# A windowed-attention, dense-layer and eight-expert kernel: row gathers issued three steps sooner, gate values copied out, 32-row tails computed in float32 in four column quarters, weight splits on VectorE alone

## The chip, the cores and the metric

The kernel runs on one core of a Trainium2 chip. The metric is the device time of one execution in microseconds; a kernel's time is the median of its runs. TensorE is written PE in the profile, its weight loads PEld, VectorE is DVE, ScalarE is ACT, GpSimd is POOL and SyncE, which issues most of the DMAs, is SP.

## What is computed

Three layers follow each other on 4 x 576 = 2304 tokens of width 512.

```
scores = scale * q @ k.T            # causal window of 64, softmax, @ v
x = concat of heads                 # [2304, 512]
h = x @ w_in                        # dense layer, width 2048
g = h * sigmoid(1.702 * h)
x = g @ w_out
logits = x @ w_gate                 # eight experts, the best one per token
gate_w = softmax(logits)[best]
for e in range(8):
    xe = x[best == e]
    out[best == e] = gate_w * (relu(xe @ w1[e]) @ w2[e])   # width 1024
```

All inputs and outputs are float32, and the kernel keeps nearly that precision: a float32 operand is split into a high part in the matmul type float32r and a low part, the rest, in the same type, and a product is made of three float32r matmuls (high by high, high by low, low by high).

## The kernel before

**Attention and the dense layer** fill the first 535 us or so, in nine chunks of 256 tokens; their order comes from a small planner with cost figures. While they run, each token's row (512 values of x, its gate value and its token number, 514 floats) is scattered into a buffer `xbuf` in DRAM, where each expert has its own stretch of rows.

**The experts** are the part that the change touches. The experts are taken in descending order of their number of tokens, with fixed room `CAPS` (L39) of 384, 352, 352, 288, 288, 256, 256 and 256 rows; below, "expert 3" is the fourth in that order. Which expert that is, is a value read at run time (`which`, L598). The room is cut into blocks of 128 rows (`blocks`, L595), so that experts 1 and 2 have a last block of 96 rows and experts 3 and 4 a last block of 32 rows.

For each expert, `load_rows` (L625) fetches its rows from `xbuf` into a tile `xg` by one DMA per block on the SP queue. There are two such tiles, one for even and one for odd experts (`xp2["go"[e % 2]]`, each with one buffer), so the rows of expert e+1 overwrite those of expert e-1. `rows_t` (L639) transposes a block on PE into `et` in PSUM, and ACT and DVE split it into `eh` and `el`; DVE also copies the token numbers into `ti` (L658). `load_expert` (L605) fetches an eighth of an expert's weights (512 KB) into a staging tile `ws`, of which there are four, and `prep_expert` (L620) splits half of such an eighth: ACT writes the high part (L150), and the low part (L151) is made on POOL for the first half and on DVE for the second. The split weights lie in tiles `whi` and `wlo` of the pool `wp`, eight of each (L69), that is two experts' worth.

`e_up` (L660) makes one of the eight 128-wide slices m of the hidden layer for all rows of the expert: 12 matmuls, whose moving operand has as many columns as the expert has rows. ACT makes `gh` from it (L681), and DVE makes `gl` (L682). `e_down` (L689) multiplies that slice by 128 rows of w2 and adds to one PSUM bank `o` per block, by three matmuls of 512 columns for each block, whatever the number of rows in the block (L162, L163 and L165). After slice 7, `e_out` (L707) scales each block by the gate value, which it reads in `xg` (L712), on ACT or, for block 1, on DVE, and scatters the rows to the output by an indirect DMA on POOL. The output tiles `os` come from a pool with three buffers (L67). PSUM has eight banks, one pool for all.

**The order** is written out by hand for PE alone (`manual_schedule`, L1025): PE runs the instructions in the order of the program. In the expert loop the other engines' queues and the DMA queue are ordered by the framework's scheduler, which follows the program's order where its own model says that an instruction is ready. The loop (L1068) has one step for each expert and slice; step (e, z) is

```
if i % NF == 0 and e + 1 < E:
    load_rows(e + 1)
e_up(*steps[i])
if i > 1:
    e_down(*steps[i - 2][0:2])
```

and after that come `rows_t` of expert e+1 for block z-2, `prep_expert` for eighth z of expert e+1, and `load_expert` two eighths further on. So `e_down` runs two steps behind `e_up`: slice 7 of expert e is finished in step (e+1, 1), its blocks are put out there, and the first transposes of the expert after next stand in step (e+1, 2). Expert 0 is special: seven of its slices were already made for its first 256 rows within the dense layer's end, and its first eight steps do the rest.

Of the kernel before, what the change touches and what calls it, by code (L numbers as in the profile page):

```python
# [9 lines left out]
F32 = mybir.dt.float32  # L10
# [3 lines left out]
U32 = mybir.dt.uint32  # L14
# [3 lines left out]
ALU = mybir.AluOpType  # L18
# [23 lines left out]
PAIR = 3  # L42
ROW = DM + 2
XB = (NT - CMIN) // P
NEG = -8.0e9
SKIP = 4096
Z_SCALE = 2.0**-29 * (1.0 - 2.0**-20)
# [4 lines left out]
def tile_model(  # L52
# [539 lines left out]
    ev_t = {}  # L592
    xp2 = {}

    def blocks(e):  # L595
        return [(b, min(P, CAPS[e] - b * P)) for b in range(-(-CAPS[e] // P))]

# [22 lines left out]
    def prep_expert(e, i, h, lo_eng):  # L620
        j, z = divmod(i, 2)
        hi, lo = ew_t[e, j]
        split(hi[:, 2 * z + h], lo[:, 2 * z + h], st_t[e, i][:, h], lo_eng)

    def load_rows(e, which_blocks=None):  # L625
        if e not in ex_t:
            ex_t[e] = [
                xp2["go"[e % 2]].tile([P, CAPS[0] // P, ROW], F32, tag="xg", name="xg", bufs=1),
                sm.tile([P, CAPS[0] // P], U32, tag="ti", name="ti"),
            ]  # L630
        xg = ex_t[e][0]
        for b, n in which_blocks or blocks(e):
            src = xbuf.rearrange("(e r) d -> e r d", e=E)[which(e), b * P : b * P + n, :]
            ins = nc.sync.dma_start(out=xg[0:n, b, :], in_=src.rearrange("o r d -> r (o d)"))
            for w in put[-2:]:
                tc.add_manual_dep(ins.ins, w.name, SYNC, reason="rows written before")
        return ins

    def rows_t(e, b):  # L639
        pool = xp2["go"[e % 2]]  # L640
        if b == 0:
            ex_t[e] += [
                pool.tile([P, KD, CAPS[0]], F32R, tag="eh", name="eh", bufs=1),
                pool.tile([P, KD, CAPS[0]], F32R, tag="el", name="el", bufs=1),
            ]
        xg, ti, eh, el = ex_t[e]
        n = blocks(e)[b][1]
        t = ps.tile([P, KD, P], F32, tag="ps", name="et")
        for k in range(KD):
            nc.tensor.transpose(  # L650
                t[:, k, 0:n], xg[0:n, b, k * P : k * P + P], ident[0:n, 0:n]
            )
        hv = eh[:, :, b * P : b * P + n]
        nc.scalar.activation(out=hv, in_=t[:, :, 0:n], func=AF.Copy)  # L654
        nc.vector.tensor_tensor(  # L655
            out=el[:, :, b * P : b * P + n], in0=t[:, :, 0:n], in1=hv.bitcast(F32), op=ALU.subtract
        )
        nc.vector.tensor_copy(out=ti[0:n, b : b + 1], in_=xg[0:n, b, DM + 1 : ROW])  # L658

    def e_up(e, m, c0=0, c1=None, skip=0):  # L660

        c1 = c1 or CAPS[e]
        n = c1 - c0
        hi, lo = ew_t[e, 2 * (m // 4)]
        f0 = (m % 4) * P
        xg, ti, eh, el = ex_t[e]
        h = ps.tile([P, 512], F32, tag="ps", name="eh_ps")[:, 0:n]
        for k in range(KD):
            mm3(
                h,  # L670
                (hi[:, k, f0 : f0 + P], lo[:, k, f0 : f0 + P]),
                (eh[:, k, c0:c1], el[:, k, c0:c1]),
                k == 0, k == KD - 1,
            )
        if "o" in xp2:
            pool, w, n_b = xp2["o"], CAPS[0], 3
        else:
            pool, w, n_b = gp, CH, 3
        gh = pool.tile([P, w], F32R, tag="gh", name="gh", bufs=n_b)[:, 0 : n - skip]
        gl = pool.tile([P, w], F32R, tag="gl", name="gl", bufs=n_b)[:, 0 : n - skip]  # L680
        nc.scalar.activation(out=gh, in_=h[:, skip:], func=AF.Relu)  # L681
        nc.vector.scalar_tensor_tensor(  # L682
            out=gl, in0=h[:, skip:], scalar=0.0, in1=gh.bitcast(F32), op0=ALU.max, op1=ALU.subtract
        )
        g_t["e", e, m] = (gh, gl, c0 + skip, c1)

    eo_t = {}

    def e_down(e, m):  # L689
        done, rows = [], []  # L690
        gh, gl, c0, c1 = g_t.pop(("e", e, m))
        hi, lo = ew_t[e, 2 * (m // 4) + 1]
        for b, n in blocks(e):
            if not c0 <= b * P < c1:
                continue
            if (e, b) not in eo_t:
                eo_t[e, b] = [ps.tile([P, DM], F32, tag="ps", name="o"), 0]
            o, i = eo_t[e, b]
            eo_t[e, b][1] += 1
            if i == NF - 1:  # L700
                done.append(b)
            rows.append((o[0:n], slice(b * P - c0, b * P - c0 + n), i == 0, i == NF - 1))
        mm3_rows(rows, (gh, gl), (hi[:, m % 4, :], lo[:, m % 4, :]))
        for b in done:
            e_out(e, b)

    def e_out(e, b):  # L707
        xg, ti = ex_t[e][0:2]
        n = blocks(e)[b][1]
        o = eo_t[e, b][0][0:n]  # L710
        os_ = yp.tile([P, ROW], F32, tag="ys", name="os")[0:n, 0:DM]
        gate = xg[0:n, b, DM : DM + 1]  # L712
        if b == 1:
            nc.vector.tensor_scalar(out=os_, in0=o, scalar1=gate, scalar2=None, op0=ALU.mult)
        else:
            nc.scalar.activation(out=os_, in_=o, func=AF.Copy, scale=gate)
        ins = nc.gpsimd.indirect_dma_start(  # L717
            out=out[:, :],
            out_offset=bass.IndirectOffsetOnAxis(ap=ti[0:n, b : b + 1], axis=0),
            in_=os_,  # L720
            in_offset=None,
            bounds_check=NT - 1,
            oob_is_err=False,
        )

        tc.declare_no_dep(ins.ins, group="out", reason="rows of their own")
        tc.add_to_no_dep_group("out", ins.ins)
# [297 lines left out]
    with tc.manual_schedule(engines={mybir.EngineType.PE}):  # L1025
        consts_attn()
        consts_gate()
        marks = {}
        for s in (slot[0, NM - 1], slot[0, NM - 1] - 3, LAST - 1, BEGIN, MEND):
            sched[s]  # L1030
        for s in sorted(x for x in sched if x < END1):
            if s == slot[0, NM - 1]:
                load_gate()
            if s == slot[0, NM - 1] - 3:
                with tc.issue_after(last_w[0].ins):
                    init_xbuf(yp.tile([P, ROW], F32, tag="ys", name="zt"))
            if s == LAST - 1:
                at_cm.__exit__(None, None, None)
                p2_cm = tc.tile_pool(name="p2g", bufs=2, reuse_waits="tile")
                xp2["g"] = p2_cm.__enter__()  # L1040
            if s == BEGIN:
                staged = tc.manual_schedule(
                    engines={
                        mybir.EngineType.Activation, mybir.EngineType.DVE, mybir.EngineType.Pool
                    }
                )
                staged.__enter__()
            if s == MEND:
                staged.__exit__(None, None, None)
            for _, fn in sorted(sched[s], key=lambda x: x[0]):  # L1050
                fn()
        xpool_cm.__exit__(None, None, None)
        yt_cm.__exit__(None, None, None)
        rows = load_rows(0, blocks(0)[2:])
        cnt, rank = pick_order()
        gp_cm.__exit__(None, None, None)
        p2o_cm = tc.tile_pool(name="p2o", bufs=1, side="right", reuse_waits="tile")
        xp2["o"] = p2o_cm.__enter__()
        for b, _ in blocks(0)[2:]:
            rows_t(0, b)  # L1060
        count_rows(cnt, rank)
        with tc.issue_after(rows.ins):
            for i in range(2):
                load_expert(1, i)
        steps = [(0, m, 0, CAPS[0], 0) for m in range(SPLIT, NF)]
        steps += [(0, m, CAPS[0] - 256, CAPS[0], 256 - (CAPS[0] - CH)) for m in range(SPLIT)]
        steps += [(e, m, 0, CAPS[e], 0) for e in range(1, E) for m in range(NF)]
        for i in range(E * NF + 2):  # L1068
            e = i // NF
            if e < E:  # L1070
                if i % NF == 0 and e + 1 < E:
                    load_rows(e + 1)
                e_up(*steps[i])
            if i > 1:
                e_down(*steps[i - 2][0:2])
            if e < E and e + 1 < E:
                z = i % NF
                if 0 <= z - 2 < len(blocks(e + 1)):
                    rows_t(e + 1, z - 2)
                prep_expert(e + 1, z, 0, nc.gpsimd)  # L1080
                prep_expert(e + 1, z, 1, nc.vector)
            if i + 2 < (E - 1) * NF:
                load_expert(*divmod(i + 2 + NF, NF))
        p2_cm.__exit__(None, None, None)
        p2o_cm.__exit__(None, None, None)
# [56 lines left out]
```

## Time and profile before

| | us |
|---|---|
| median of 3 runs (lowest to highest) | 769.55 (767.17 to 771.27) |
| the profiled execution | 768.63 |
| its span, first to last instruction | 766.9 |
| PE busy in the span | 730.2 (95%) |
| DVE, ACT, POOL busy | 477.5, 370.7, 171.2 |

The span is what the profile covers; 1.7 us of the profiled execution lie outside it. Busy time is the time in which at least one instruction of an engine was running. A matmul's end is modelled, and matmuls overlap, so the distance from one matmul's start to the next one's start says more than the mean duration.

### The profile page before, as it was taken

How to read it: one execution, taken by the hardware profiler on the slowest of the kernel's cores; microseconds unless marked ns; L12 is line 12 of the kernel's file. 1: busy time of each engine (PE TensorE's matmuls, PEld its weight loads, DVE VectorE, ACT ScalarE, POOL GpSimd, SP SyncE). 2: the span in 40 equal slices, each digit the busy share in tenths (PEclk: the TensorE clock that was granted, in tenths of full speed). 3: DMA queues.
4: the chain of work that ended last, by engine and by line, in shares of the span. 5: the costliest groups of instructions: out<-in, count | busy, mean ns of one | idle time of the engine just before them, and what ended most of it. 6: DMA issues, size and time to landing. Idle time of an engine off the chain costs nothing. (4 is left out here: it accounts for less than half of the span.)

```text
span 766.9 us, 14568 instructions
## 1 busy us (share of the span) xinstructions
PE 730.2 (95%) x5372; PEld 639.3 (83%) x5373; DVE 477.5 (62%) x1408; ACT 370.7 (48%) x965; POOL 171.2 (22%) x153
## 2 busy tenths in 40 slices
PE   5779999999999999999999999989999999999996
PEld 3669888888988898889888988868898888888895
DVE  5999866946764845936747538463765637265641
ACT  5999674444344344535443522451563526345520
POOL 2000011120112021011110110241554626255531
PEclk9899999999999999999999999999999999999998
DMA  9992278130222112211220000441862717437520
GB/s 343 385 383 92 101 271 289 37 101 18 84 74 100 41 49 86 73 37 65 74 100 1 1 28 1 141 135 42 282 230 98 271 56 250 164 115 264 189 68 24
DMA packets 43195, 98.97 MB, mean 129 GB/s; under 512 B 3823, under 2 KB 12015, under 8 KB 42864
## 3 DMA queue, kind: packets, MB, share of 16 engines
q1 hardware_dynamic: 40128, 88.54, 33.6%
q0 software_dynamic: 2992, 9.46, 3.2%
q8 instruction: 43, 0.70, 0.4%
q14 instruction: 32, 0.26, 0.1%
HBM read 82.22 MB, written 16.03 MB: 128 GB/s over the span
## 5 line engine op out<-in xcount | busy, mean ns | idle before, releaser
L155 PE MATMUL h<-xh,whi 128*128 128x256 f32 x576 | 166.0, 288 | 0.0
L157 PE MATMUL h<-xh,wlo 128*128 128x256 f32 x576 | 163.8, 284 | 0.1
L156 PE MATMUL h<-xl,whi 128*128 128x256 f32 x576 | 163.7, 284 | 0.0
L162 PE MATMUL y<-whi,gh 128*128 128x512 f32 x288 | 119.0, 413 | 5.0 <-ACT gh L397 5.0
L390 DVE SCALAR_TENSOR_TENSOR th<-th,h 128x256 f32<-128x256 f32 x144 | 60.1, 417 | 100.4 <-ACT th L386 99.5
L386 ACT ACTIVATE th<-h 128x256 f32<-128x256 f32 x144 | 54.7, 381 | 134.7 <-PE h L157 129.5
L155 PEld LDWEIGHTS h<-xh,whi 128*128 128x128 f32 x576 | 110.8, 192 | 6.2 <-ACT whi L364 0.3
L156 PEld LDWEIGHTS h<-xl,whi 128*128 128x128 f32 x576 | 110.8, 192 | 4.7
L163 PE MATMUL y<-wlo,gh 128*128 128x512 f32 x288 | 114.7, 398 | 0.0
L151 POOL TENSOR_TENSOR wlo<-ws,whi 128x512 fp32r<-128x512 f32 x64 | 94.3, 1485 | 87.5 <-ACT whi L150 82.9
L157 PEld LDWEIGHTS h<-xh,wlo 128*128 128x128 f32 x576 | 110.7, 192 | 0.5 <-DVE wlo L369 0.5
L151 DVE TENSOR_TENSOR wlo<-ws,whi 128x512 fp32r<-128x512 f32 x64 | 87.1, 1368 | 33.8 <-ACT whi L150 32.2
L238 POOL TENSOR_TENSOR pr<-pr,su 128x512 f32<-128x512 f32 x28 | 31.1, 1111 | 297.6 <-DVE su L236 177.7
L150 ACT ACTIVATE whi<-ws 128x512 fp32r<-128x512 f32 x128 | 74.4, 625 | 41.2 <-DMA ws<-in_w 40.8
L397 ACT ACTIVATE gh<-th 128x256 fp32r<-128x256 f32 x144 | 60.1, 417 | 65.2 <-DVE th L390 63.9
L165 PE MATMUL y<-whi,gl 128*128 128x512 f32 x288 | 90.7, 396 | 0.2
L447 DVE CUSTOM_DVE_ANT_0 junk<-ys,wg 128x512 bf16<-128x512 f32 x128 | 89.1, 696 | 2.7 <-DMA wg<-in_w_gateT 1.2
L155 PE MATMUL eh_ps<-eh,whi 128*128 128x256 f32 (+3 forms) x284 | 85.2, 300 | 0.7 <-ACT eh L654 0.7
L156 PE MATMUL eh_ps<-el,whi 128*128 128x256 f32 (+3 forms) x284 | 83.6, 294 | 0.3 <-DVE el L655 0.3
L157 PE MATMUL eh_ps<-eh,wlo 128*128 128x256 f32 (+3 forms) x284 | 83.5, 294 | 0.0
L403 DVE TENSOR_TENSOR gl<-th,gh 128x256 fp32r<-128x256 f32 x144 | 61.5, 427 | 25.2 <-ACT gh L397 21.7
L162 PEld LDWEIGHTS y<-whi,gh 128*128 128x128 f32 x288 | 54.8, 190 | 15.5 <-ACT gh L397 7.9
(128 smaller groups left out, 1223.6 us busy)
## 6 DMA issues: line engine op xcount, KB each, us to landing
ws<-in_w SPq DMA_DIRECT2D x64, 512.0 KB, 5.1
qkv<-in_qkv SPq DMA_DIRECT2D x36, 672.0 KB, 4.9
st<-in_w_in SPq DMA_DIRECT2D x16, 512.0 KB, 3.6
st<-in_w_out SPq DMA_DIRECT2D x16, 512.0 KB, 11.1
xbuf<-zt SPq DMA_DIRECT2D x8, 771.0 KB, 10.9
xg<-xbuf SPq DMA_DIRECT2D x17, 257.0 KB, 3.3
wg<-in_w_gateT SPq DMA_DIRECT2D x2, 1024.0 KB
xg<-xbuf SPq DMA_DIRECT2D x2, 192.8 KB, 4.2
```

Of the source, the lines that this page charges most:

```text
L150: nc.scalar.activation(out=hi, in_=raw, func=AF.Copy)
L151: lo_eng.tensor_tensor(out=lo, in0=raw, in1=hi.bitcast(F32), op=ALU.subtract)
L155: nc.tensor.matmul(out=o, lhsT=a[0], rhs=b[0], start=first, stop=False)
L156: nc.tensor.matmul(out=o, lhsT=a[0], rhs=b[1], start=False, stop=False)
L157: nc.tensor.matmul(out=o, lhsT=a[1], rhs=b[0], start=False, stop=last)
L162: nc.tensor.matmul(out=o, lhsT=a[0][:, s], rhs=b[0], start=first, stop=False)
L163: nc.tensor.matmul(out=o, lhsT=a[0][:, s], rhs=b[1], start=False, stop=False)
L165: nc.tensor.matmul(out=o, lhsT=a[1][:, s], rhs=b[0], start=False, stop=last)
L390: nc.vector.scalar_tensor_tensor(out=th, in0=th, scalar=1.0, in1=h_t.pop((c, m)), op0=ALU.add, op1=ALU.mult)
L397: nc.scalar.activation(out=gh, in_=th, func=AF.Copy)
L403: nc.vector.tensor_tensor(out=gl, in0=th, in1=gh.bitcast(F32), op=ALU.subtract)
L447: nc.vector.tensor_tensor_reduce(out=junk, in0=ys[:, 0:DM], in1=wg_t[e // 4][:, e % 4, :], scale=1.0, scalar=0.0, op0=ALU.mult, op1=ALU.ad ...
```

## The change

Five things change, all in the expert stage.

- **Gate values.** `rows_t` copies a block's gate column into a small tile `ga` beside `ti`, and `e_out` reads it there, so that `xg` is no longer read by `e_out`.
- **Rows.** `load_rows(e + 1)` at step (e, 0) becomes `load_rows(e + 2)` at step (e, 5); `load_rows(1)` moves ahead of the first two loads of expert 1's weights.
- **Tails.** For experts 3 and 4 (288 rows), `e_up` still makes all 288 columns, but the last 32 go through a `max` with zero on DVE into a float32 tile `gt`, and `gh`, `gl` and `e_down` have 256 columns. After slice 7, `down_tail` makes the 32-row block by 8 float32 matmuls: slice i of each half of the hidden layer writes to PSUM partitions 32i to 32i+31 of one bank. `out_tail` adds the four quarters (one ACT copy, three DVE adds), scales and scatters them.
- **Raw weights.** For these matmuls w2 of the expert is fetched a second time, unsplit, by `load_raw` at steps 5 and 6 (four DMAs of 512 KB on SP), into one more `whi` and one more `wlo` tile.
- **Splits.** For experts 1 to 7 the two halves of an eighth are split by one ACT and one DVE instruction of 1024 columns; POOL makes no low parts any more. Expert 0 keeps the old way.

```diff
+TAIL = 32
+    def tail(e):
+        return CAPS[e] % P if CAPS[e] % P == TAIL else 0
+    def prep_both(e, i):
+        j, z = divmod(i, 2)
+        hi, lo = ew_t[e, j]
+        split(hi[:, 2 * z : 2 * z + 2], lo[:, 2 * z : 2 * z + 2], st_t[e, i], nc.vector)
     def load_rows(e, which_blocks=None):
         if e not in ex_t:
             ex_t[e] = [
                 xp2["go"[e % 2]].tile([P, CAPS[0] // P, ROW], F32, tag="xg", name="xg", bufs=1),
-                sm.tile([P, CAPS[0] // P], U32, tag="ti", name="ti"),
             ]
+            tg = sm.tile([P, 2, CAPS[0] // P], F32, tag="ti", name="ti")
+            ex_t[e] += [tg[:, 0, :].bitcast(U32), tg[:, 1, :]]
...
         nc.vector.tensor_copy(out=ti[0:n, b : b + 1], in_=xg[0:n, b, DM + 1 : ROW])
+        nc.vector.tensor_copy(out=ga[0:n, b : b + 1], in_=xg[0:n, b, DM : DM + 1])
...
+        if tail(e):
+            n -= TAIL
+            if m == 0:
+                gt_t[e] = xp2["o"].tile([P, NF, TAIL], F32, tag="gt", name="gt", bufs=1)
+            nc.vector.tensor_scalar_max(gt_t[e][:, m, :], h[:, n:], 0.0)
+            h = h[:, 0:n]
...
-        g_t["e", e, m] = (gh, gl, c0 + skip, c1)
+        g_t["e", e, m] = (gh, gl, c0 + skip, c0 + n)
+    def load_raw(e, j):
+        raw = raw_t[e, j] = wp.tile([P, 4, 512], F32, tag=("whi", "wlo")[j], name="raw")
+        for z in range(2):
+            r = j * 512 + 2 * z * P
+            src = w2[which(e), r : r + 2 * P, :]
+            nc.sync.dma_start(
+                out=raw[:, 2 * z : 2 * z + 2], in_=src.rearrange("o (k p) f -> p (o k) f", p=P)
+            )
+    def down_tail(e):
+        b = CAPS[e] // P
+        o = ps.tile([P, DM], F32, tag="ps", name="ot")
+        for j in range(2):
+            for i in range(4):
+                nc.tensor.matmul(
+                    out=o[TAIL * i : TAIL * i + TAIL], lhsT=gt_t[e][:, 4 * j + i, :],
+                    rhs=raw_t[e, j][:, i, :], start=(j == 0), stop=(j == 1),
+                )
+        eo_t[e, b] = [o, NF]
+    def out_tail(e):
+        b = CAPS[e] // P
+        o = eo_t[e, b][0]
+        ti, ga = ex_t[e][1:3]
+        a, os_ = [yp.tile([P, ROW], F32, tag="ys", name="os")[0:TAIL, 0:DM] for _ in range(2)]
+        nc.scalar.activation(out=a, in_=o[0:TAIL], func=AF.Copy)
+        for i in range(1, 4):
+            nc.vector.tensor_tensor(out=a, in0=o[TAIL * i : TAIL * i + TAIL], in1=a, op=ALU.add)
+        nc.scalar.activation(out=os_, in_=a, func=AF.Copy, scale=ga[0:TAIL, b : b + 1])
+        put_out(os_, ti[0:TAIL, b : b + 1])
...
-        gate = xg[0:n, b, DM : DM + 1]
+        gate = ga[0:n, b : b + 1]
...
         with tc.issue_after(rows.ins):
+            load_rows(1)
             for i in range(2):
                 load_expert(1, i)
...
             if e < E:
-                if i % NF == 0 and e + 1 < E:
-                    load_rows(e + 1)
                 e_up(*steps[i])
             if i > 1:
                 e_down(*steps[i - 2][0:2])
+            f = (i - 2) // NF
+            if i > 1 and tail(f) and (i - 2) % NF == NF - 1:
+                down_tail(f)
+                out_tail(f)
+            if e < E and tail(e) and i % NF in (5, 6):
+                load_raw(e, i % NF - 5)
             if e < E and e + 1 < E:
                 z = i % NF
                 if 0 <= z - 2 < len(blocks(e + 1)):
                     rows_t(e + 1, z - 2)
-                prep_expert(e + 1, z, 0, nc.gpsimd)
-                prep_expert(e + 1, z, 1, nc.vector)
+                prep_both(e + 1, z)
+            if i % NF == NF - 3 and e + 2 < E:
+                load_rows(e + 2)
             if i + 2 < (E - 1) * NF:
                 load_expert(*divmod(i + 2 + NF, NF))
```

`put_out`, not shown, is the indirect DMA that stood at the end of `e_out` (L717 to L727), now called by both.

## Rows read from the trace of the kernel before

**Rows 1.** The page's first part: busy time, share of the span, instructions.

```profile
PE 730.2 (95%) x5372; PEld 639.3 (83%) x5373; DVE 477.5 (62%) x1408; ACT 370.7 (48%) x965; POOL 171.2 (22%) x153
```

**Rows 2.** One step of expert 4 and of expert 5, by window; the columns stand first.

```profile
core 0: us, PE busy (x) PEld busy (x) DVE busy (x) ACT busy (x) POOL busy (x), PEclk, DMA share, GB/s
...
675.69:679.35 3.66, 3.66 (x23) 3.05 (x21) 3.45 (x4) 2.02 (x5) 2.98 (x2) 1.00 1.00 379
...
703.69:706.51 2.82, 2.82 (x19) 2.56 (x18) 2.82 (x3) 1.56 (x4) 2.82 (x3) 1.00 0.60 215
```

**Rows 3.** What PE waited for from 540 us on: total us, times, longest.

```profile
PE et L650 <- DMA xg<-xbuf: 4.1, 5, 1.6
```

**Rows 4.** PE in order of time, expert 6 to 7: start, us, instruction, idle before.

```profile
717.24 0.62 PE L165 MATMUL o<-whi,gl 128*128 128x512 f32 x2
719.45 0.66 PE L650 MATMUL et<-ident,xg 128*128 128x128 f32 x4 [1.59 <-DMA xg<-xbuf]
```

**Rows 5.** What SP's queue waited for, 480 us on: total, times, longest.

```profile
SPq L617 <- DVE wlo L151: 81.1, 34, 6.9
SPq L634 <- DVE os L714: 72.7, 5, 17.3
```

**Rows 6.** PE in order of time: one step of expert 3.

```profile
648.48 0.30 PE L155 MATMUL eh_ps<-eh,whi 128*128 128x288 f32 x1
...
650.07 0.39 PE L162 MATMUL o<-whi,gh 128*128 128x512 f32 x1
...
651.45 0.86 PE L165 MATMUL o<-whi,gl 128*128 128x512 f32 x3
652.14 0.30 PE L155 MATMUL eh_ps<-eh,whi 128*128 128x288 f32 x1
```

**Rows 7.** Groups by line and shape: the matmuls of the 32-row blocks.

```profile
L165 PE MATMUL o<-whi,gl 128*32 128x512 f32 x16 | 6.3, 396 | 0.0
L163 PE MATMUL o<-wlo,gh 128*32 128x512 f32 x16 | 6.3, 395 | 0.0
L162 PE MATMUL o<-whi,gh 128*32 128x512 f32 x16 | 6.3, 393 | 0.0
```

**Rows 8.** PE in order of time: float32 matmuls in array parts (scores, then attention by values).

```profile
186.41 1.10 PE L203 MATMUL s<-qkv 64*64 64x128 f32 x32
211.49 0.69 PE L261 MATMUL t<-pr,qkv 128*64 128x64 f32 x16
```

**Rows 9.** Groups by line and shape: the same matmuls' counts and mean durations.

```profile
L261 PE MATMUL t<-pr,qkv 128*64 128x64 f32 x576 | 25.5, 233 | 6.5 <-ACT pr L252 6.5
L203 PE MATMUL s<-qkv 64*64 64x128 f32 x576 | 24.0, 302 | 8.2 <-DMA qkv<-in_qkv 8.2
```

**Rows 10.** Groups by line and shape: splits and other two-input work on DVE, POOL, ACT.

```profile
L151 POOL TENSOR_TENSOR wlo<-ws,whi 128x512 fp32r<-128x512 f32 x64 | 94.3, 1485 | 87.5 <-ACT whi L150 82.9 <-PE h L157 3.1 <-PE eh_ps L157 1.0
L151 DVE TENSOR_TENSOR wlo<-ws,whi 128x512 fp32r<-128x512 f32 x64 | 87.1, 1368 | 33.8 <-ACT whi L150 32.2 <-issue 1.2
L150 ACT ACTIVATE whi<-ws 128x512 fp32r<-128x512 f32 x128 | 74.4, 625 | 41.2 <-DMA ws<-in_w 40.8
L403 DVE TENSOR_TENSOR gl<-th,gh 128x256 fp32r<-128x256 f32 x144 | 61.5, 427 | 25.2 <-ACT gh L397 21.7 <-PE y L165 2.9
L369 DVE TENSOR_TENSOR wlo<-st,whi 128x512 fp32r<-128x512 f32 x32 | 21.0, 682 | 0.1
L350 ACT ACTIVATE st<-st 128x1024 f32<-128x1024 f32 x16 | 18.6, 1161 | 1.5 <-DVE st L342 1.3
L716 ACT ACTIVATE os<-o,xg 32x512 f32<-32x512 f32 x2 | 1.3, 664 | 0.0
L658 DVE CAST ti<-xg 128x1 uint32<-128x1 f32 x17 | 2.6, 152 | 20.4 <-DMA xg<-xbuf 20.4
```

**Rows 11.** DMA issues, 556 to 740 us: count, KB each, median us to landing.

```profile
ws<-in_w SPq DMA_DIRECT2D x47, 512.0 KB, 4.6
...
out<-os,ti POOLq DMA_INDIRECT x15, 6.1
```

More of the change, by code (lines that the diff above doesn't have):

```diff
@@ L645, in rows_t @@
             ]
-        xg, ti, eh, el = ex_t[e]
+        xg, ti, ga, eh, el = ex_t[e]
         n = blocks(e)[b][1]
@@ L665, in e_up @@
         f0 = (m % 4) * P
-        xg, ti, eh, el = ex_t[e]
+        eh, el = ex_t[e][3:5]
         h = ps.tile([P, 512], F32, tag="ps", name="eh_ps")[:, 0:n]
@@ L684, in e_up @@
         )
-        g_t["e", e, m] = (gh, gl, c0 + skip, c1)
+        g_t["e", e, m] = (gh, gl, c0 + skip, c0 + n)
+    gt_t = {}
+    raw_t = {}
+    def load_raw(e, j):
[26 more added lines that the diff above has]
+        put_out(os_, ti[0:TAIL, b : b + 1])
     eo_t = {}
@@ L707, in e_out @@
     def e_out(e, b):
-        xg, ti = ex_t[e][0:2]
+        ti, ga = ex_t[e][1:3]
         n = blocks(e)[b][1]
@@ L716, in e_out, with put_out @@
             nc.scalar.activation(out=os_, in_=o, func=AF.Copy, scale=gate)
+        put_out(os_, ti[0:n, b : b + 1])
+    def put_out(os_, rows):
         ins = nc.gpsimd.indirect_dma_start(
             out=out[:, :],
-            out_offset=bass.IndirectOffsetOnAxis(ap=ti[0:n, b : b + 1], axis=0),
+            out_offset=bass.IndirectOffsetOnAxis(ap=rows, axis=0),
             in_=os_,
```

## The prediction

> **What bounds the kernel now.** I read the page first: PE is busy for 95% of the span, and every other engine far less [rows 1]. Then I took single steps of the expert stage by window: in the steps of experts 4 and 5 PE is busy for all of the time, at the full granted clock, 1.00 or 2.4 GHz [rows 2]. So a gain can come from two places alone: fewer or shorter matmuls, or less waiting by PE. The view of waits shows the second: from 540 us on PE waits five times, each time in the transposes of `rows_t` for the rows of `xg`, 4.1 us in all [rows 3]. In order of time the longest looks like this: the last matmul of an expert's output starts at 717.47 (two from 717.24, 0.23 apart), and the transposes start at 719.45 [rows 4]. Why the rows are late is seen in the DMA queue: SP stands at `load_rows` (L634) until `e_out` has read the old gate values, 72.7 us in five waits [rows 5]; `e_out` comes in step (e, 1) and the transposes in step (e, 2). That SP, with the weight loads behind it, can stand there for up to 17.3 us without PE ever waiting for a weight says how far the weights are ahead.
>
> **Tails: what goes.** One step of expert 3 runs from 648.48 to 652.14: 12 up matmuls of 288 columns take 1.59, then 9 down matmuls of 512 columns take 2.07, 0.23 each, three of them for the 32 rows [rows 6]. There are 48 such matmuls in the run [rows 7], so 48 x 0.23 = 11.0 us of PE goes. A step becomes 1.59 + 6 x 0.23 = 2.97.
>
> **Tails: what comes.** The nearest rows are the float32 matmuls of the attention. Their code issues 8 per unit for 36 units, and the trace has 576 records: a float32 matmul is two records [rows 9]. The scores run in four 64 by 64 parts: 32 records of 128 columns in 1.10 us with a last one of 0.30, so (1.10 - 0.30)/31 = 26 ns each [rows 8, 9]. One after the other that would be 0.20 ns a column, less than half of a float32r matmul's 0.23 us for 512; so four do run abreast, and four take 0.103 us, 0.81 ns a column. A tail is 8 matmuls, 16 records of 512 columns: four abreast 4 x 512 x 0.81 = 1.66 us. No row has four column quarters fed by 128 rows; the two column halves of the attention by values take (0.69 - 0.23)/15 = 31 ns for 64 columns, 61 a pair, so two abreast for certain [rows 8, 9]. Two abreast a tail would take 3.3, one at a time 6.6. I take four abreast, as the halves already run side by side with data of their own, with 0.2 for entry and exit: 2 x 1.86 = 3.7 us. Below 3.4 nothing in the rows allows. Net: 3.7 - 11.0 = -7.3; ends -7.6 and +2.2.
>
> The Trainium skill, "TensorE: Matmul & The Clock Gate", Part 3, gives measured speedups at 512 columns of 3.07 for four row tiles and 2.38 for three column tiles, not four and three. An estimate by 3.07 instead of 4 makes a tail 2.16 and the sum 757.4 instead of 756.4. "TensorEngine Tiling (Array Packing)", Key Properties, adds that a change of tiling mode drains the engine; no row here prices it, and the term of 0.2 stands without it.
>
> **Rows three steps sooner.** The gate copy frees `xg` after the transposes, so the load at step (e, 5) waits for nothing and has five steps, some 14 us, for what now lands in 4 to 5 (a weight DMA of twice the size takes 4.6 [rows 11]). The five waits go. Each cost more than its wait: the transposes of rows 4 start 1.75 us after their turn at 717.70, with a wait of 1.59, so 0.16 more each: 4.1 + 0.8 = 4.9 us. Ends 0 and 4.9. Next late would be nothing: `e_up` of the new expert comes six steps later. The load passes two weight loads in SP's queue and delays them by its 0.5 to 0.8 MB, about 2 us at 379 GB/s [rows 2]; the lead of up to 17 us covers it. `load_rows(1)`, moved ahead of two weight loads, likewise.
>
> **Gate copies.** 21 more DVE instructions of about 0.15 [rows 10], 3.2 us in all, beside PE. At the same time the DVE's 20.4 us of standing at the token copy for late rows goes [rows 10].
>
> **Splits.** DVE's low parts take 1368 ns beside POOL, and 682 for the same shape in the dense layer, where POOL makes none [rows 10]. From 256 to 512 columns that is 427 to 682, so 1024 columns cost 682 + 2 x 255 = 1.19 us, less than DVE spends on its half now; bounds 1.19 and 2 x 1.37 = 2.74. I take 1.19, as POOL's part ends. ACT's one instruction costs 1.16 by L350, against 2 x 0.62 now [rows 10]. DVE then has per step of expert 5: 1.19 + 0.42 for `gl` + about 0.3 (four to five instructions of 0.7 an expert) = 1.9 of 2.82. All of it stays beside PE: zero.
>
> **Tail's side work.** Per slice a `max` of 0.15 on DVE; per tail two ACT instructions of 0.66 and three adds of some 0.7 on DVE [rows 10], 3.5 us in a chain. What they hold up is `gl` and `gh` behind them in the queues; the cover is the two steps between `e_up` and `e_down`, 2.97 + 1.38 + 1.59 = 5.9 us. Two new waits lie there. `gt` has one buffer: expert 4's first `max` waits for expert 3's tail in step (4, 1); if DVE's queue holds `gl` behind it, 0.15 + 0.43 remain to do in the 1.59 of `e_up` before `e_down` asks for it. And `os` has three buffers for four tiles: the last waits for a scatter, 6.1 us to landing [rows 11], with ACT behind. I cost both at zero, with a microsecond at most to spare. The tail also holds one PSUM bank instead of the eight steps of a third `o`.
>
> **Raw weights.** Four DMAs per tail, 2.1 MB, on SP. By rotation expert 4's copy falls on the slot of its own first half of w2, read until step (4, 5). From there to the tail it is 2 x 2.97 + 2 x 2.82 = 11.6 us. Ahead or within lie 2.1 MB raw, 0.5 MB rows, 0.5 MB weights: 3.1 MB at 379 GB/s are 8.2 us. Cost zero, with 3 us to spare.
>
> **Sum.** -7.3 - 4.9 = -12.2 against the profiled execution's own 768.6 (span 766.9 and 1.7 around it): 756.4, and I write 756.5. The median of the three runs is 0.9 above that execution, and the runs spread by 4 us, so I keep it. About 0.5%, 3.8 us, is what a measurement of this kernel can tell from no change.
>
> **The rivals.**
>
> *The raw copy is late.* If three more staged weight loads (1.6 MB, 4.1 us) go ahead of it, it lands up to 2 us after its turn; if SP also stands at its slot, 4. For: DMA is at share 1.00 in the step of expert 4 already [rows 2]. Against: the mean there is far lower, and expert 3's slot is free two steps earlier. Two tails: 4 to 8 us given back, 760.5 to 764.5; a wait for `gl` or a bank near the tail would give the same size. Chance 0.22.
>
> *The quarters don't run side by side.* One at a time a tail takes 6.6 + 0.2: 13.6 - 11.0 = +2.6, and with the rows' -4.9 it is 766.3, the same within the measurement; two abreast, 759.7. Against: the halves. Chance 0.08 for the first.
>
> *The rows still wait.* If the change does not do what it says for the rows, because another wait holds SP at them, only the tails count: 761.3. Against: nothing but `e_out` is named for those five waits [rows 5]. Chance 0.05.
>
> *VectorE becomes the bound, and the kernel is slower.* In the step of expert 5 DVE and POOL are both busy for all 2.82 us [rows 2]. If the split keeps its stretched price of 2.74, DVE needs 2.74 + 0.42 + 0.3 = 3.5 in a step of 2.82 and 3.7 in one of 2.97 with the `max`. Then the splits fall behind in experts 3 to 6: 16 x 0.7 + 16 x 0.7 = 22 us, less the 12.2: 779. It decides where a 1024-column split costs more than 2.82 - 0.72 = 2.1 us. For: no row shows this shape. Against: the stretch goes with POOL's work, by 682 against 1368. Chance 0.05.
>
> **How the numbers follow.** Forecast 0.60, the rivals 0.22, 0.08, 0.05 and 0.05. Faster by over 0.5% (under 765.7): 0.60 + 0.22 + 0.05, less 0.04 for several of these at once: 0.83. Same: the quarters one at a time and what I took off: 0.12. Slower: 0.05. The range goes down to 753 (both terms in full at the low end, 768.6 - 7.6 - 4.9 = 756.1, and the runs' spread of some 2 to 3 us below) and up to 765, which takes in the late copy and the rows that wait and leaves out the quarters one at a time, VectorE and the lower tail, under 0.2 together.
>
> **What would show it.** PE's wait for `xg` gone from the waits; SP no longer at `e_out` in its queue's waits; a tail as 16 records in about 1.9 us, right after slice 7, with no wait before it; a step of experts 3 and 4 of 2.97 instead of 3.66; a 1024-column split of about 1.2 on DVE with POOL down to its scatters; DMA share higher in experts 3 and 4 alone. I am wrong if PE waits for the raw tile, for `gl` or for a weight split in experts 3 to 6, if a tail takes over 3 us, or if DVE's split costs over 2.1.

## The result and the profile after

The changed kernel takes 756.18 us (median of 6 runs, 753.90 to 757.56), against 768.55 for the kernel before in 6 runs (766.78 to 771.27). The ratio is 0.9831, with a 95% interval of 0.9812 to 0.9850. The forecast was 756.5, and the profiled execution took 757.56 with a span of 755.8. That forecast and median lie 0.3 us apart is luck: the six runs alone spread over 3.7 us.

The first part of the page, to be set beside [rows 1]:

```profile
PE 720.1 (95%) x5356; PEld 632.8 (84%) x5357; DVE 474.4 (63%) x1451; ACT 366.1 (48%) x911; POOL 90.9 (12%) x97
```

PE's share is the same 95%, as work and waits went together. POOL lost 80 us, and DVE, which took that work over, became no busier.

The sum is best read from the expert stage. Here is the window from the first 384-column `e_up` matmul to the last expert's first `os`, in the kernel before and then in the changed one. Behind the stretch and its length stand the busy times of PE, PEld, DVE, ACT and POOL, then the granted clock, the DMA share and GB/s.

```profile
536.65:759.57 222.92, 218.48 (x1302) 190.10 (x1302) 121.80 (x182) 101.40 (x207) 102.55 (x75) 1.00 0.50 171
```

```profile
537.39:748.49 211.10, 210.44 (x1286) 185.94 (x1286) 118.32 (x222) 96.37 (x152) 22.25 (x19) 1.00 0.59 200
```

The stage is 11.82 us shorter: 218.48 - 210.44 = 8.04 less of PE's work, and 4.44 - 0.66 = 3.78 less idle time of PE. The prediction had 12.2: 7.3 for the tails and 0.16 a wait beyond the waits themselves, together 8.1 of work, and 4.1 of waiting. The stage started 0.74 later, so the span is 11.1 shorter. That lies in the dense layer, which the change leaves nearly alone: 0.42 had come about earlier, and 0.32 comes with the first of the two waits for `gl` below.

What PE waited for from 520 us on (total, times, longest), for [rows 3]:

```profile
PE o L166 <- DVE gl L699: 0.8, 2, 0.5
PE eh_ps L156 <- ACT eh L664: 0.7, 1, 0.7
PE eh_ps L157 <- DVE el L665: 0.3, 1, 0.3
```

The waits for `xg` are gone. The lower two rows, 1.0 us, stood in the kernel before as well. The first row is new. The transposes now start as soon as PE's queue comes to them, here 0.46 behind the start of two down matmuls, where [rows 4] had 2.21:

```profile
661.84 0.62 PE L166 MATMUL o<-whi,gl 128*128 128x512 f32 x2
662.30 0.60 PE L660 MATMUL et<-ident,xg 128*128 128x128 f32 x4
```

The first of the two waits for `gl` lies just ahead of the window. DVE's queue stood at the token copy until the first expert's rows had landed, and the `gl` came behind it:

```profile
534.69 0.15 DVE L668 CAST ti<-xg 128x1 uint32<-128x1 f32 x1 [4.00 <-DMA xg<-xbuf]
534.82 0.41 DVE L699 SCALAR_TENSOR_TENSOR gl<-eh_ps,gh 128x256 fp32r<-128x256 f32 x1
```

```profile
535.29 0.73 PE L166 MATMUL o<-whi,gl 128*128 128x512 f32 x2 [0.46 <-DVE gl L699]
```

The token copy stood there in the kernel before too, and its `gl` was just in time. The new gate copy adds some 0.07 to it; the rest is rows that landed later against PE, for without the gate copy there are such waits of 0.32 and 0.53 in two experiments below (the tails alone, the earlier load alone).

What SP's queue waited for from 480 us on, three of the rows, for [rows 5]:

```profile
SPq L621 <- DVE wlo L152: 79.2, 35, 7.3
...
SPq L712 <- PE o L166: 12.4, 1, 12.4
...
SPq L712 <- PE ot L722: 4.8, 1, 4.8
```

No row names an output tile `os` at the rows' load (L644) any more. Two of the raw loads (L712) stand at slots that PE still reads, one of them at expert 3's tail, and PE waited for neither.

PE in order of time around the first tail:

```profile
653.43 0.61 PE L166 MATMUL o<-whi,gl 128*128 128x512 f32 x2
653.98 1.92 PE L722 MATMUL ot<-raw,gt 128*32 128x512 f32 x16
655.83 0.40 PE L156 MATMUL eh_ps<-eh,whi 128*128 128x288 f32 x1
```

From the tail's first matmul to the next matmul behind it is 655.83 - 653.98 = 1.85 us, for 16 records; 1.86 was predicted. The second tail took the same, within 0.01.

One step of expert 3 and one of expert 5 by window (columns as above), for [rows 6] and [rows 2]:

```profile
645.01:647.97 2.96, 2.96 (x20) 2.71 (x18) 2.28 (x3) 2.18 (x3) 0.00 (x0) 1.00 0.66 239
697.24:700.06 2.82, 2.82 (x19) 2.56 (x18) 1.38 (x3) 1.31 (x3) 0.00 (x0) 1.00 0.66 198
```

The step of expert 3 is 2.96 (2.97 predicted). In expert 5's, DVE is busy for 1.38 of 2.82 where it was busy throughout.

Groups by line and shape, for [rows 10]; behind the bar stand busy us, mean ns of one, and the idle time before:

```profile
L152 DVE TENSOR_TENSOR wlo<-ws,whi 128x1024 fp32r<-128x1024 f32 x56 | 67.8, 1220 | 25.6 <-ACT whi L151 25.4
...
L735 DVE TENSOR_TENSOR os<-ot,os 32x512 f32<-32x512 f32 x6 | 4.1, 686 | 0.2
L668 DVE CAST ti<-xg 128x1 uint32<-128x1 f32 x17 | 2.4, 148 | 15.6 <-DMA out<-os,ti 9.8 <-DMA xg<-xbuf 5.8
L669 DVE COPY ti<-xg 128x1 f32<-128x1 f32 x17 | 2.3, 143 | 0.0
```

A 1024-column low part takes 1.22 us (1.19 predicted), less than a 512-column one took beside POOL, 1.37.

### The profile page after: what moved, and what is told of

It is laid out like the page before. It is cut to its first block, busy times and chain, and to the rows that moved or that the text cites. A ratio compares the mean times of both kernels' runs of the same rounds, so it can differ in the third digit from the quotient of the medians.

```text
span 755.8 us, 14418 instructions
## 1 busy us (share of the span) xinstructions
PE 720.1 (95%) x5356; PEld 632.8 (84%) x5357; DVE 474.4 (63%) x1451; ACT 366.1 (48%) x911; POOL 90.9 (12%) x97
## 5 line engine op out<-in xcount | busy, mean ns | idle before, releaser
L152 DVE TENSOR_TENSOR wlo<-ws,whi 128x1024 fp32r<-128x1024 f32 (+1 forms) x64 | 77.7, 1222 | 34.1 <-ACT whi L151 33.7
L151 ACT ACTIVATE whi<-ws 128x1024 fp32r<-128x1024 f32 (+1 forms) x72 | 68.0, 960 | 40.9 <-DMA ws<-in_w 30.6
L166 PEld LDWEIGHTS y<-whi,gl 128*128 128x128 f32 x288 | 53.9, 189 | 14.9 <-DVE gl L404 2.8
```

What stands on the lines that cost most here:

```text
L151: nc.scalar.activation(out=hi, in_=raw, func=AF.Copy)
L152: lo_eng.tensor_tensor(out=lo, in0=raw, in1=hi.bitcast(F32), op=ALU.subtract)
L166: nc.tensor.matmul(out=o, lhsT=a[1][:, s], rhs=b[0], start=False, stop=last)
```

## The experiments

Each line gives the median against that of the kernel before on the same chip (770.11 for the first four, 770.27 for the next four, 770.16 for the last two), and the ratio with its interval. The intervals are 0.2 to 0.4% to either side. The times that the expectations name start from 768.5 or 756.2, so it is the ratios that compare with them.

**The rows alone** (gate copy and earlier load).

```
 the change, with
-    def tail(e): return CAPS[e] % P if CAPS[e] % P == TAIL else 0
+    def tail(e): return 0
-    prep_both(e + 1, z)
+    prep_expert(e + 1, z, 0, nc.gpsimd); prep_expert(e + 1, z, 1, nc.vector)
```

> Gate copies and rows three steps sooner; tails and splits as before. The forecast's theory (two terms that add, rows 4.9 us and tails 7.3 us, splits nothing): PE's five waits for the rows are gone and the time is 768.5 - 4.9 = 763.6 us. Rival (the rows' waits are paid by the low parts: with POOL and DVE still sharing them, PE waits for gl or weights instead): 766 to 768.5 us, with those waits in the list.

Measured: 766.28, ratio 0.9944 (0.9925 to 0.9963), about 4.3 us less by the ratio where the prediction had 4.9; the interval, 2.8 to 5.8 us, takes in both. The waits for `xg` are gone, but PE has another one, in expert 0's short steps. PE, DVE and POOL in order of time, and by window the stretch behind the wait:

```profile
554.28 0.50 PE L166 MATMUL o<-whi,gl 128*128 128x512 f32 x1 [1.54 <-DVE gl L699]
```

```profile
549.32 4.70 DVE L152 TENSOR_TENSOR wlo<-ws,whi 128x512 fp32r<-128x512 f32 x1
553.95 0.28 DVE L699 SCALAR_TENSOR_TENSOR gl<-eh_ps,gh 128x128 fp32r<-128x128 f32 x1
```

```profile
549.68 3.79 POOL L152 TENSOR_TENSOR wlo<-ws,whi 128x512 fp32r<-128x512 f32 x3
```

```profile
554.28:556.00 1.72, 1.72 (x13) 1.67 (x14) 1.72 (x2) 0.44 (x2) 1.12 (x1) 1.00 0.16 45
```

One low part on DVE lasted 4.70 us, while POOL did three in a row, and the `gl` that PE wanted stood behind it. The clock stayed at 1.00. So the trace shows the waits that the rival named, though the times alone don't decide. In this execution something else cost as much: where the expert stage begins, the clock fell, as the last section shows.

**The tails alone** (the rows' load and the gate as before, splits as before).

```
 the change, with
-    load_rows(1)                                        # ahead of the loop
+    if i % NF == 0 and e + 1 < E: load_rows(e + 1)      # at the head of the step
-    if i % NF == NF - 3 and e + 2 < E: load_rows(e + 2)
-        nc.vector.tensor_copy(out=ga[...], ...)
-    gate = ga[0:n, b : b + 1]                           # and likewise in out_tail
+    gate = xg[0:n, b, DM : DM + 1]
 and prep_expert twice, as above
```

> The float32 tails in four column quarters and the second load of w2; rows, gate values and splits as before. The forecast's theory: 768.5 - 7.3 = 761.2 us, each tail about 1.9 us, the five waits for the rows still there. Rival (the raw copy needs SP's queue free of the wait at the rows, else it is late): a wait for the raw tile before a tail and 763 to 767 us.

Measured: 774.36, ratio 1.0044 (1.0022 to 1.0065): slower, which neither theory had. The tails themselves are as in the whole change (3.8 us for 32 records), and PE waits for no raw tile. What PE and SP waited for from 540 us on:

```profile
PE et L660 <- DMA xg<-xbuf: 11.6, 5, 4.7
```

```profile
SPq L644 <- DVE os L765: 46.8, 3, 18.0
SPq L644 <- ACT os L735: 35.0, 2, 18.6
```

After experts 3 and 4 the rows' load now stands at L735, the last instruction of `out_tail` ahead of its scatter, which reads the old gate values behind a chain of an ACT copy and three DVE adds. ACT in order of time shows that chain's ends, SP that the load goes out right behind it, and PE what came of it:

```profile
657.70 0.59 ACT L732 ACTIVATE os<-ot 32x512 f32<-32x512 f32 x1 [0.93 <-PE ot L721]
...
662.16 0.72 ACT L735 ACTIVATE os<-os,xg 32x512 f32<-32x512 f32 x1 [0.33 <-DVE os L734]
```

```profile
662.90 0.90 SPq L644 DMA_DIRECT2D xg<-xbuf  x2
```

```profile
660.37 0.63 PE L166 MATMUL o<-whi,gl 128*128 128x512 f32 x2
665.68 1.12 PE L660 MATMUL et<-ident,xg 128*128 128x128 f32 x4 [4.67 <-DMA xg<-xbuf]
...
667.07 0.44 PE L158 MATMUL eh_ps<-eh,wlo 128*128 128x288 f32 x1
667.31 0.44 PE L156 MATMUL eh_ps<-eh,whi 128*128 128x288 f32 x1
```

The matmuls behind the wait are 0.24 apart; the same shape goes at 0.13 in [rows 6], 12 of them in 1.59. The windows of the wait, of what follows, of the next 3 us, and of the stretch behind the second such wait (3.76 us), give the clock:

```profile
660.84:665.68 4.84, 0.17 (x1) 0.00 (x1) 1.60 (x4) 1.10 (x2) 0.87 (x1) 0.91 0.48 140
665.68:671.87 6.19, 6.19 (x23) 5.61 (x23) 2.66 (x6) 3.05 (x6) 2.25 (x2) 0.52 1.00 351
671.87:675.00 3.13, 3.13 (x22) 2.97 (x21) 2.44 (x6) 2.99 (x7) 2.17 (x3) 1.00 0.72 274
698.58:703.43 4.85, 4.85 (x22) 4.48 (x23) 1.19 (x4) 2.03 (x5) 0.72 (x1) 0.65 0.98 335
```

After the 4.67 us in which PE did nothing, the granted clock is 0.52, near the lower level of 1.2 GHz, for 6.2 us, and then 1.00 again. The account: the first place loses 4.84 us until the transposes start and 6.19 x (1 - 0.52) = 3.0 by the clock, the second 3.9 and 4.85 x (1 - 0.65) = 1.7. That is 13.4, against 0.66 and 1.46 lost at the same two places before, so 11.3 more; less the tails' 7.3 this makes +4.0. The waits at the other three places differ by +0.9 together, so +4.9; the profiled executions lie 5.4 apart (774.04 and 768.63), and by the ratio it is +3.4. The clock's share is worked out so from the windows; no run tried it by itself.

**The splits alone.**

```
 before, with
-    prep_expert(e + 1, z, 0, nc.gpsimd)
-    prep_expert(e + 1, z, 1, nc.vector)
+    prep_both(e + 1, z)
```

> Splits of 1024 columns on VectorE alone; rows, gate values and tails as before. The forecast's theory: the same, 768.5 us, within 1 us, with a split at about 1.2 us and POOL idle but for its scatters. Rival A (the splits beside POOL held something up, so that their relief is part of the gain): 764 to 767 us. Rival B (a long split stands in front of gl on DVE, and PE pays for it everywhere): 770 us or more.

Measured: 769.52, ratio 0.9991 (0.9975 to 1.0007): no change that this measurement can tell. A 1024-column low part takes 1.22 us here too; the waits for `xg` are still there (4.3 us), and from 530 us on PE waits for no `gl`.

**All but the tails.**

```
 the change, with
-    def tail(e): return CAPS[e] % P if CAPS[e] % P == TAIL else 0
+    def tail(e): return 0
```

> The whole change without the tails (rows sooner, gate copies, splits on VectorE alone). The forecast's theory: 763.6 us, as with the rows alone. Rival (DVE's splits and the rows need each other): more than 1.5 us away from the run with the rows alone, to either side.

Measured: 764.58, ratio 0.9921 (0.9896 to 0.9945), 6.1 us less. The 1.54 us wait for `gl` of the first experiment is not there; one of 0.5 is left. Against the rows alone the difference is 0.23% with intervals that overlap, so it is the trace, not the times, that shows what the splits add. The tails are then worth 0.9921 - 0.9831 = 0.90%, 6.9 us, give or take 2.4 by the two intervals.

**The whole change without the earlier load.**

```
 the change, with
-    load_rows(1)                                        # ahead of the loop
+    if i % NF == 0 and e + 1 < E: load_rows(e + 1)
-    if i % NF == NF - 3 and e + 2 < E: load_rows(e + 2)
```

> The whole change but for the move: rows are loaded at step (e, 0) again, with the gate copies, tails and splits of the change. What the tails alone did (slower, as the rows' load waited for the tail's last reader of the gate in xg) suggests that the gate copy, not the three steps, is what matters. Theory now: the load waits for no reader of xg, is issued at about step (e, 0) and lands before step (e, 2): 757 to 758 us, at most a microsecond of waits for xg. Rival (two steps are too few for a load behind the raw and weight loads in SP's queue): 760 us or more, with waits for xg back in the list.

Measured: 757.38, ratio 0.9826 (0.9799 to 0.9853), the same as the whole change. From 540 us on PE waits for nothing at all. So, with the gate copy, the load may stay at step (e, 0).

**The earlier load alone**, without the gate copy, the tails and the new splits.

```
 the change, with tail(e) = 0, prep_expert twice as above, and
-        nc.vector.tensor_copy(out=ga[0:n, b : b + 1], in_=xg[0:n, b, DM : DM + 1])
-        gate = ga[0:n, b : b + 1]
+        gate = xg[0:n, b, DM : DM + 1]
```

> The kernel before with the load of the rows moved to step (e, 5) but no gate copy: e_out still reads xg. Theory: nothing is gained, as the load still waits for e_out's last reader: 769 to 771 us, with the five waits for xg as before and SP standing at the rows for longer, weights behind it. Rival (the place in SP's queue is what makes the rows late): 764 to 766 us.

Measured: 771.46, ratio 1.0007 (0.9990 to 1.0024): nothing. What SP and then PE waited for from 540 us on, one row of SP's and two of PE's:

```profile
SPq L644 <- DVE os L765: 75.6, 5, 17.7
```

```profile
PE o L166 <- DVE gl L698: 3.1, 3, 2.2
PE et L660 <- DMA xg<-xbuf: 2.9, 3, 1.2
```

SP stands at the load for as long as in [rows 5]; the instruction is earlier in the queue, and what frees the tile is not. The waits for `xg` did fall, from 4.1 to 2.9, and waits for `gl` of 3.1 took their place, with the splits still shared with POOL. The two experiments together show that the move is not needed beside the gate copy and gains nothing without it; the gate copy by itself, with the old splits and without tails, was not run.

**One quarter at a time, and two abreast.** All partial sums in the same 32 rows of PSUM, or in two stretches of 32, with fewer adds behind them.

```
 the change, one at a time:
-    out=o[TAIL * i : TAIL * i + TAIL], ... start=(j == 0), stop=(j == 1),
+    out=o[0:TAIL], ... start=(j == 0 and i == 0), stop=(j == 1 and i == 3),
-    for i in range(1, 4):        # the adds
+    for i in range(0):
 two abreast:
+    out=o[TAIL * (i % 2) : TAIL * (i % 2) + TAIL], ... start=(j == 0 and i < 2), stop=(j == 1 and i > 1),
+    for i in range(1, 2):
```

> The whole change, but all eight float32 matmuls of a tail go to the same 32 columns and PSUM rows, one after the other, and the adds fall away. Theory (in the change four run abreast): a tail takes 6.6 to 7.0 us instead of 1.83, so 756.2 + 2 x 5.0 = 766.2 us. Rival (the trace's starts mislead and the quarters are served in turn anyway): 756 us again.

> The whole change, but a tail's matmuls use two of the four column quarters. Theory: two abreast, a tail takes 3.3 to 3.6 us, so 756.2 + 2 x 1.7 = 759.6 us. Rival (the quarters are served in turn): as with one quarter.

Measured: 766.85, ratio 0.9957 (0.9939 to 0.9974), and 760.21, ratio 0.9870 (0.9843 to 0.9898). PE around the first tail, one at a time and then two abreast:

```profile
658.45 7.05 PE L722 MATMUL ot<-raw,gt 128*32 128x512 f32 x16
665.43 0.40 PE L156 MATMUL eh_ps<-eh,whi 128*128 128x288 f32 x1
```

```profile
653.32 3.63 PE L722 MATMUL ot<-raw,gt 128*32 128x512 f32 x16
656.87 0.40 PE L156 MATMUL eh_ps<-eh,whi 128*128 128x288 f32 x1
```

From a tail's first matmul to the next matmul behind it is 6.98 us one at a time, 3.55 two abreast and 1.85 in the whole change, so four abreast run 3.8 times as fast as one at a time. By the ratios the two kernels lie 9.7 and 3.0 us above the whole change. The Trainium skill, "TensorE: Matmul & The Clock Gate", Part 3, states 2.38 for three column tiles and 3.07 for four row tiles; these four column tiles, in float32, do better than that.

**The old splits in the whole change.**

```
 the change, with
-    prep_both(e + 1, z)
+    prep_expert(e + 1, z, 0, nc.gpsimd); prep_expert(e + 1, z, 1, nc.vector)
```

> The whole change, but the splits of the weights made by halves as before, one low part on POOL and one on DVE. Theory: nearly the same, 757 to 758 us; alone, the splits on VectorE were worth nothing, but with the rows sooner and the old splits PE waited 1.55 us for a gl behind a stretched low part in expert 0's short steps, so about that wait comes back. Rival A (no part of the gain): 756.2 us with no such wait. Rival B (POOL's stretch is what the tails' adds and the max on DVE cannot bear): 760 us or more, with waits for gl in experts 3 to 5.

Measured: 758.58, ratio 0.9858 (0.9824 to 0.9892); the interval overlaps that of the whole change, so the times can't tell them apart. The trace does: what PE waited for from 530 us on, one such wait in PE's order of time, DVE at that place, and the clock behind it.

```profile
PE o L166 <- DVE gl L699: 4.2, 3, 1.9
```

```profile
700.95 0.50 PE L166 MATMUL o<-whi,gl 128*128 128x512 f32 x1 [1.95 <-DVE gl L699]
```

```profile
695.29 4.61 DVE L152 TENSOR_TENSOR wlo<-ws,whi 128x512 fp32r<-128x512 f32 x2
```

```profile
701.29:705.00 3.71, 3.71 (x17) 3.46 (x16) 1.90 (x4) 0.78 (x2) 0.49 (x2) 0.54 0.75 195
```

The `gl` in question stood behind these two low parts, a split of the new expert's rows and a copy. The waits are 4.2 us where the whole change has 0.8, and behind the longest of them, in expert 5, the clock is 0.54 for 3.7 us. In this execution the old splits so cost 3.4 us of waits and 3.71 x (1 - 0.54) = 1.7 by the clock, some 5 us. But it took 763.27, near the upper end of the six runs (757.24 to 763.79); by the ratios the difference is about 2 us, not clear of noise.

**The two small copies on POOL**, an attempt at a version better than both.

```
 the change, with
-        nc.vector.tensor_copy(out=ti[...], ...)
-        nc.vector.tensor_copy(out=ga[...], ...)
+        nc.gpsimd.tensor_copy(out=ti[...], ...)
+        nc.gpsimd.tensor_copy(out=ga[...], ...)
```

> The whole change, with the copies of token numbers and gate values on POOL, which is idle now, instead of DVE. A try at a faster version: in the change PE waits 0.5 and 0.4 us for a gl that stands behind such copies, or behind long splits, on DVE. Theory: the first of these waits goes, 755.5 us, which can't be told from 756.2 by time, but in the list of waits. Rival (a copy on POOL waits for the scatters before it and holds up the next ones, and os runs out): 757 us or more.

Measured: 755.89, ratio 0.9836 (0.9796 to 0.9876). Both waits of the changed kernel for `gl` are gone from the list, and the time can't be told from that of the change. The first stood behind these copies; why the second went as well was not followed up.

## Why the prediction was right, and where it was not

**Tails: right in both terms.** 48 matmuls went, and a step is 2.96 instead of 3.66. A tail is 1.85 by the trace, so the entry and exit cost about the 0.2 allowed beside the 1.66 worked out. The experiments with fewer quarters give the same terms from the other side: against four abreast, 9.9 us more were worked out for one at a time and 9.7 measured, 3.3 and 3.0 for two abreast. The choice among the bounds, four abreast from a row of two halves, is thereby shown; it was an argument before. The estimate by the page's 3.07, 757.4, lies inside the runs' spread and only the length of the tail decides against it.

**Rows: the amount right, the reason half right.** All five waits went, and the transposes start at their turn, so the 0.16 beyond each wait went too. That fits the stage's account (8.04 and 3.78), which is 0.4 short of the 12.2: about the second of the waits for `gl`, 0.38. But the prediction gave the gain to the gate copy and the five steps of lead together. The load may stay where it was (757.38), and moved alone it brings nothing (771.46).

**Splits: "zero" holds alone, and by the traces not beside the rows.** Taken alone they are zero, as the prediction had it. Beside the rows, with POOL still splitting, PE waits for `gl` 4.2 us in the whole change and 2.2 with the rows alone, against 0.8 and 0.5 with the new splits; some 0.5 of each is the wait just ahead of the stage. The times go the same way, by 0.27% and 0.23%, with intervals that overlap: that the splits are worth some 2 us there is likely, not shown. The prediction credited 4.9 for the rows as if that did not rest on DVE being quick, and the cover it named, 1.9 of 2.82 in a step, is that of the new splits. So the sum came out because the whole was priced with all three parts; the terms of 4.9 and 7.3 were not prices for each part alone.

**What is late next: not nothing.** The prediction wrote that after the rows nothing would be late. A `gl` is, twice, by 0.46 and 0.38 us. The second stands behind a 1.22 us low part in expert 0's short steps, the first behind the small copies, which waited for `xg`, and of these the token copy is an old one; on POOL they cost PE no wait. DVE also still stands at the token copies for 15.6 us, where the prediction had its 20.4 go: 9.8 of them wait for a scatter that reads the old token numbers. The prediction costed `gl` only around the tails, where it was covered.

**The raw copy: right by luck of place.** The slots were not those that the prediction worked out. Expert 3's copy waited for a slot of w2 that expert 2's last `e_down` reads, and expert 4's for the slot that expert 3's tail holds. Both loads still landed before PE asked: no wait for `raw` stands in PE's rows above. SP sent them some three steps before steps 5 and 6, where the loop names them: expert 4's from 655.1 to 659.4, with at most 9.7 us to landing, and its tail starts at 680.31. So they had 11 us to spare where the prediction had 3.

**The rivals.** One quarter at a time and VectorE as the bound are ruled out by 1.85 and 1.22 us. The rival in which the rows still wait was priced at 761.3, the tails' gain alone. The nearest run to its condition is the one with the tails alone, where the gate is still read in `xg`, and its time was 774.36: the price left out that a tail itself can make the rows later, when its chain holds the old gate values. That is a way to a slower kernel that the prediction did not have: without the gate copy the tails lose more than they gain.

## What to carry to other kernels

A transfer into a reused buffer starts when the buffer's last reader has run: a copy of the few values that are read late is worth more than an earlier issue, and whatever is put ahead of that last reader delays the transfer. Parts of a change are not a sum: the tails cost 3.4 us alone and gained 6.9 beside the rest. Price each part with the others in place and with them away, above all where one part lengthens a chain that another one takes off the path. A product of 32 output rows can use the whole array by giving each quarter of the columns its own share of the inner dimension, here in 1.85 us instead of 7.0.

## What the runs showed of the hardware that was not expected

The stretch of a low part beside POOL has no fixed size. Least, median and longest duration in ns of the same instruction on DVE, in the kernel before and in the whole change with the old splits:

```profile
L151 DVE TENSOR_TENSOR wlo<-ws,whi x64: 851/1362/1789, 493.1 to 733.8; 128x512 fp32r<-128x512 f32 x64
```

```profile
L152 DVE TENSOR_TENSOR wlo<-ws,whi x64: 670/1346/5591, 494.9 to 714.5; 128x512 fp32r<-128x512 f32 x64
```

The medians are the same and the longest is three times as long; in the rows-alone run the one of 4.70 us stood beside POOL's three without a pause. It is such long ones that a `gl` behind them meets. The Trainium skill, "GPSIMD Engine Reference", Key points, says that POOL shares its SBUF interfaces with VectorE, in contention with VectorE's instructions that have two SBUF inputs; the traces agree (0.68 us alone, a median of 1.36 beside POOL), and with POOL's splits gone a part of twice the width takes 1.22.

The granted clock fell to 0.52 behind a PE wait of 4.67 us and to 0.54 behind one of 1.95, each for several us, while it stayed at 1.00 behind the 1.54 of the rows-alone run. So a wait can cost nearly twice its length (1.95 and 1.7 by the clock), and the list of waits does not show the second half. Nor does the length of one wait tell by itself. Here are the start of the expert stage and what follows, in the rows-alone run and then in the whole change:

```profile
533.00:536.80 3.80, 2.21 (x11) 0.98 (x9) 2.34 (x12) 0.60 (x1) 0.00 (x0) 1.00 0.00 0
536.80:540.00 3.20, 3.20 (x10) 3.20 (x11) 2.69 (x16) 0.00 (x0) 0.00 (x0) 0.51 0.23 56
```

```profile
534.32:538.12 3.80, 2.38 (x11) 1.07 (x10) 2.33 (x12) 0.60 (x1) 0.00 (x0) 1.00 0.00 0
538.12:541.32 3.20, 3.20 (x22) 3.20 (x23) 3.03 (x17) 0.49 (x1) 0.00 (x0) 1.00 0.23 53
```

In the rows-alone run three waits, the longest of 0.69 us, came close together, and the clock fell to 0.51 for 3.2 us, which costs 1.6. In the whole change nearly the same waits at that place left it at 1.00. What makes the difference these runs do not show.
